# Sums of four heads' exponentials in one matmul of 228 columns instead of four of 57

## The chip, the cores and the metric

One Trainium2 chip, one of its cores. The metric is device time in microseconds (us). Several runs are quoted as a median with their lowest and highest value.

## The reference

Two attention blocks read the same input `x` (2048 positions, 1024 features, 32 heads of 32), and a gate mixes them. The change touches only block B, a sliding attention over eight positions, two apart:

```python
W, dil = 8, 2
idx = pos[:, None] - off[None, :]            # off = 0, 2, ..., 14
logits = einsum("bhsd,bhswd->bhsw", q, kg) * scale   # masked where idx < 0
attn = softmax(logits, axis=-1)
o = einsum("bhsw,bhswd->bhsd", attn, vg)     # then @ wo
```

Block A (a linear attention) and the projections of both blocks are most of the work.

## The kernel before

The kernel splits the positions into even and odd ones, so a window becomes eight neighbours. It then works in 18 *fills*. A fill holds two blocks (h = 0, 1) of `nq` = 57 queries (56 in the last fill of each half) with 64 keys each, for all 32 heads. A fill has three parts on TensorE and around it:

- **S**: 64 small matmuls give the scores of 32 heads, 64 keys x 57 queries each. ScalarE takes exp of all of them, VectorE multiplies by a mask, into `E`. `E` has 64 keys of each block on 64 partitions, and its columns are ordered by head: 57 for each.
- **PV**: two groups (g = 0, 1) of 16 heads. Each head's 64 values (64 x 32) are multiplied by its exponentials, and a 64 x 32 block of ones is multiplied by the same exponentials to give the sum of each query, repeated on 32 partitions.
- ScalarE takes Ln and Exp(-x) of the sums, VectorE multiplies.

The array of 128 x 128 is used as eight tiles of 64 x 32: `tile_position=(64 * h, 32 * j)`.

```python
def each(e, g=g):                       # one PV group: 64 matmuls
    for o in range(2):                  # 0: values, 1: sums
        for c in range(4):
            for h in range(2):
                for j in range(4):
                    hd = 16 * g + 4 * c + j
                    w = vt[64*h:64*h+64, hd*32:hd*32+32] if o == 0 else ones[64*h:64*h+64, :]
                    last = e.matmul(SO[2*g+h].ap((4*o+c)*nq, (4*o+c+1)*nq)[32*j:32*j+32, :], w,
                                    E[64*h:64*h+64, (8*j+4*g+c)*nq:(8*j+4*g+c+1)*nq],
                                    start=True, stop=True, tile_position=(64*h, 32*j))
    return last
P.op("pe", each, 0.35, mode="c", ...)   # 0.35: the planner's cost, in us
# ... then Ln, Exp(-x) on ScalarE and the product on VectorE, for this g
```

Each `e.matmul` becomes two instructions, a weight load and a matmul; I call them a *pair*. Each `P.op` is one step of a plan. A list scheduler orders all steps when the kernel is built, from the costs given; the last instruction of a step signals a semaphore. A column index of `E` and of the sums in PSUM shows the opening: for fixed j and g the four heads c = 0..3 lie side by side in both.

Of the kernel before, what the change touches and what calls it, by code (L numbers as in the profile page):

```python
# [1102 lines left out]
def build_kernel(nc, A_x, A_wqkv, A_wo, B_x, B_wqkv, B_wo, gate_w, out):  # L1103
# [10 lines left out]
    def SB(shape, dtype, name, at=None):  # L1114
        n = SZ[dtype]
        for d in shape[1:]:
            n *= d
        if at is None:
            at = base[0]
            base[0] += (n + 31) // 32 * 32  # L1120
        uid[0] += 1
        h = nc.alloc_sbuf_tensor_at("%s_%d" % (name, uid[0]), list(shape), dtype, offset=at)
        return Tile("S", h, at, list(shape), dtype)
# [35 lines left out]
    def hb(p0, p1, half):  # L1159
        return [("H%d" % half, p0, p1, None)]  # L1160

    xT = SB([128, 8, S], BF16, "xT")
    qT = SB([128, 8, S], BF16, "qT")
    kT = SB([128, 8, S], BF16, "kT")
# [3 lines left out]
    ones = SB([128, 32], BF16, "ones")  # L1168
# [7 lines left out]
    g = SB([128, NT], F32, "g")  # L1176
# [46 lines left out]
    def plan(seen):  # L1223

        P = Prog(nc, nc.alloc_semaphore)
# [94 lines left out]
        def group(bank, lhs, rhs, reads, lo=0, hi=8):  # L1320
            def fn(e):
                last = None
                for dc in range(lo, hi):
                    last = e.matmul(bank.ap(), lhs(dc), rhs(dc), start=(dc == 0), stop=(dc == 7))  # L1324
                return last
            return P.op("pe", fn, (hi - lo) * mm(512), reads=reads, writes=[bank.iv])
# [19 lines left out]
        def w_half(slot, half):  # L1346
            return (lambda dc: ws[slot][:, dc, half * 512:half * 512 + 512]), ws[slot].part((0, 8), (half * 512, half * 512 + 512))

        def w_cols(slot, j):
            return (lambda dc: ws[slot][:, dc, j * 128:(j + 1) * 128]), ws[slot].part((0, 8), (j * 128, (j + 1) * 128))  # L1350
# [17 lines left out]
        for t, half in [(4 * b + i, half) for b in range(NT // 4) for half in range(2) for i in range(4)]:  # L1368
            vt, vs = vst.next()
            xs, xr = x_tile(t)  # L1370
            bank = main.next()
            w, wr = w_half(0, half)
            step = 2 if t == 0 else 8
            for d in range(0, 8, step):
                o = group(bank, xs, w, [xr, ws[0].part((d, d + step), (half * 512, half * 512 + 512))], d, d + step)
            move(vt[:, :], bank.ap, 512, bank, vt.all())
            P.op("sp", lambda e, t=t, vt=vt, half=half: e.dma_start(vB_hbm[t * 128:(t + 1) * 128, half * 512:half * 512 + 512], vt[:, :]), 0.6, reads=[vt.all()],
                 writes=[hb(t * 128, (t + 1) * 128, half)], chan="vst%d" % vs, lat=0.5, prio=5)
# [29 lines left out]
        SO = banks[4:8]  # L1408
# [5 lines left out]
        def fill(e_, qs, nq, offs):  # L1414
            t0 = e_ * HS
            k0 = [qs + nq * h - offs[h] for h in range(2)]
            m = msk[KINDS.index((nq, offs))]
            vt, vslot = vr.next()
            for h in range(2):
                P.op("sp", lambda e, h=h: e.dma_start(vt[64 * h:64 * h + 64, :], vB_hbm[t0 + k0[h]:t0 + k0[h] + 64, :]), 0.4,  # L1420
                     reads=[hb(t0 + k0[h], t0 + k0[h] + 64, i) for i in range(2)], writes=[vt.all()], chan="v%d_%d" % (vslot, h), lat=0.5)

            def s_fn(e):
                for c in range(8):
                    for h in range(2):
                        for j in range(4):
                            last = e.matmul(SO[j].ap(c * nq, (c + 1) * nq)[64 * h:64 * h + 64, :], kT[32 * j:32 * j + 32, c, t0 + k0[h]:t0 + k0[h] + 64],  # L1427
                                            qT[32 * j:32 * j + 32, c, t0 + qs + h * nq:t0 + qs + (h + 1) * nq], start=True, stop=True, tile_position=(32 * j, 64 * h))
                return last
            P.op("pe", s_fn, 0.45, mode="r", reads=[kT.part((0, 8), (t0 + k0[0], t0 + k0[1] + 64)), qT.part((0, 8), (t0 + qs, t0 + qs + 2 * nq))],  # L1430
                 writes=[s.iv for s in SO], name="S")
            E, _ = Er.next()
            P.op("act", lambda e: e.activation(E[:, 0:32 * nq].rearrange("p (j q) -> p j q", j=4), ps[:, 4:8, 0:8 * nq], ACT.Exp), act(32 * nq),  # L1433
                 reads=[s.iv for s in SO], writes=[E.all()])
            ev = lambda: E[:, 0:32 * nq].rearrange("p (g q) -> p g q", g=16)
            P.op("dve", lambda e: e.tensor_tensor(ev(), ev(), m[:, :, :].rearrange("p r q -> p (r q)")[:, None, :].to_broadcast([128, 16, 2 * nq]), ALU.mult),
                 0.15 + 32 * nq / 1920.0, reads=[E.all(), m.all()], writes=[E.all()])

            def values():

                for g in range(2):
                    def each(e, g=g):
                        for o in range(2):
                            for c in range(4):
                                for h in range(2):
                                    for j in range(4):
                                        hd = 16 * g + 4 * c + j
                                        w = vt[64 * h:64 * h + 64, hd * 32:hd * 32 + 32] if o == 0 else ones[64 * h:64 * h + 64, :]
                                        last = e.matmul(SO[2 * g + h].ap((4 * o + c) * nq, (4 * o + c + 1) * nq)[32 * j:32 * j + 32, :], w,  # L1449
                                                        E[64 * h:64 * h + 64, (8 * j + 4 * g + c) * nq:(8 * j + 4 * g + c + 1) * nq],  # L1450
                                                        start=True, stop=True, tile_position=(64 * h, 32 * j))
                        return last
                    bi = [SO[2 * g].iv, SO[2 * g + 1].iv]
                    P.op("pe", each, 0.35, mode="c", reads=[vt.all(), ones.all(), E.all()], writes=bi, name="PV")
                    L, _ = Lr.next()
                    pb = lambda o, g=g: ps[:, 4 + 2 * g:6 + 2 * g, 4 * o * nq:4 * (o + 1) * nq]
                    P.op("act", lambda e, L=L, pb=pb: e.activation(L[:, :, 0:4 * nq], pb(1), ACT.Ln), act(8 * nq), reads=bi, writes=[L.all()])
                    P.op("act", lambda e, L=L: e.activation(L[:, :, 0:4 * nq], L[:, :, 0:4 * nq], ACT.Exp, scale=-1.0), act(8 * nq), reads=[L.all()], writes=[L.all()])  # L1458
                    P.op("dve", lambda e, L=L, pb=pb, g=g: e.tensor_tensor(  # L1459
                        qT[:, 4 * g:4 * g + 4, t0 + qs:t0 + qs + 2 * nq].rearrange("p c (h q) -> p h c q", h=2),  # L1460
                        pb(0).rearrange("p h (c q) -> p h c q", c=4), L[:, :, 0:4 * nq].rearrange("p h (c q) -> p h c q", c=4), ALU.mult), dps(8 * nq),
                        reads=bi + [L.all()], writes=[qT.part((4 * g, 4 * g + 4), (t0 + qs, t0 + qs + 2 * nq))])
            after(PVLAG, values)

        pace = [0.0]
# [3 lines left out]
        def slot(rate):  # L1469
            slot_n[0] += 1  # L1470
            while later and later[0][0] <= slot_n[0]:
                later.pop(0)[1]()
            while states and states[0][0] <= slot_n[0]:
                states.pop(0)[1]()
            pace[0] = min(pace[0] + rate, 1.0) if todo else 0.0
            if todo and pace[0] >= 1.0:
                pace[0] -= 1.0
                fill(*todo.pop(0))

        def after(n, f, cols=False):  # L1480
            later.append((slot_n[0] + n, f, cols))
            later.sort(key=lambda x: x[0])


        for e_ in range(2):
            if True:
                for j in range(8):
                    for isq in range(2):
                        for u in (2 * e_, 2 * e_ + 1):
                            bank = main.next()  # L1490
                            w, wr = w_cols(1 + isq, j)
# [38 lines left out]
        for t in range(NT):  # L1530
# [3 lines left out]
            for r in range(4):  # L1534
                bank = main.next()
                w, wr = w_half((3, 0)[r // 2], r % 2)
# [126 lines left out]
        for t in range(NT):  # L1663
            tgt, c0 = a_loc(t)
            o_, os_ = osb.next()
            e_, r = t // 8, t % 8
            parts = [(0, 512), (512, 1024)] if t < NT - 1 else [(0, 512), (512, 768), (768, 1024)]
            for f0, f1 in parts:
# [3 lines left out]
                def fn(e, t=t, bank=bank, f0=f0, f1=f1):  # L1672
# [8 lines left out]
                    reads=[bank.iv, gm.all(), tgt.part((i0, i1), (c0, c0 + 128))], writes=[o_.part((f0, f1))])  # L1681
                if t == NT - 1 or f1 == 1024:
                    c = f0 if t == NT - 1 else 0
                    P.op("sp", lambda e, e_=e_, r=r, o_=o_, c=c, f1=f1: e.dma_start(out2[e_, r * 128:(r + 1) * 128, c:f1], o_[:, c:f1]), 0.5,
                         reads=[o_.part((c, f1))], chan="out%d_%d" % (os_, c), lat=1.0)
# [13 lines left out]
    P, flag_op = best[:2]  # L1699
# [52 lines left out]
```

## Time and profile before

| | before |
|---|---|
| time, median (lowest to highest) | 510.26 us (509.35 to 511.56), 3 runs |
| span of the profiled run | 507.9 us |
| PE busy | 501.5 us, 99% |
| matmuls / weight loads | 6121 / 6121 |

The busy times of the profile's page (us, share of the span, number of instructions; PE is TensorE's matmuls, PEld its weight loads), of the kernel before:

```profile
PE 501.5 (99%) x6121; PEld 239.4 (47%) x6121; DVE 265.0 (52%) x456; ACT 196.2 (39%) x335; POOL 6.6 (1%) x30
```

The chain that ended last, from the same page, as shares of the span, first by engine and then by line:

```profile
PE 96%; SPq 2%; DMA 1%; ACT 1%; issue 0%; DVE 0%
PE ps_all L1324 75%; PE ps_all L1674 11%; PE ps_all L1449 4%; PE ps_all L1427 2%; PE ps_all L1599 1%; SPq L1294 1%; DMA w_4_52<-in_B_wqkv_dram 1%; PE ps_all L1520 1%; PE ps_all L1577 1%; SPq L1299 0%; PE ps_all L1392 0%; ACT ra_50_98 L1601 0%; ACT ra_52_100 L1601 0%; ACT ra_51_99 L1601 0%; ACT e_27_75 L1333 0%
```

TensorE bounds the kernel: 96% of the chain is its own work. Line 1324 holds the projections, 1449 PV, 1427 S.

Pieces of the chain in order of time (start, length, what; PEq and SPq are the sequencers of TensorE and SyncE, *issue* is time in which an engine waited for nothing that the profile shows), around the first fill:

```profile
127.89 0.63 PE ps_all L1427 x64
128.52 5.29 PE ps_all L1324 x24
133.81 1.17 PE ps_all L1449 x128
134.97 3.56 PE ps_all L1324 x16
```

S, then 24 matmuls of projections, then the 128 matmuls of PV without a break, then projections. The neighbours change from fill to fill, but each of the 18 has its 128 PV matmuls in one unbroken run.

Weight loads in order of time (start, length, engine, line, operands, array rows * columns, count) in the same PV.

```profile
133.74 0.19 PEld L1449 LDWEIGHTS ps_all<-E_39_87,v_43_91 64*32 64x32 bf16 x32 [0.42 <-DVE mx_55_103 L1280]
133.87 0.44 PEld L1449 LDWEIGHTS ps_all<-E_39_87,ones_58 64*32 64x32 bf16 x32
134.22 0.35 PEld L1449 LDWEIGHTS ps_all<-E_39_87,v_43_91 64*32 64x32 bf16 x32
134.52 0.35 PEld L1449 LDWEIGHTS ps_all<-E_39_87,ones_58 64*32 64x32 bf16 x32
134.90 0.76 PEld L1324 LDWEIGHTS ps_all<-xT_49,w_5_53 128*128 128x128 bf16 x5
```

A fill's PV takes from 133.74 to 134.90, the first weight load of the next projection: 1.16 us (1.166 us as the mean of 18 fills, from the single records). In the single records the steady step from one pair to the next is 8.33 ns. "S" takes 0.632 us by the same measure.

The gate, line 1392, is the one place in this kernel with wide matmuls on several tiles (durations in ns, least/median/most):

```profile
L1392 PE MATMUL ps_all<-xT_49,gwr_67 x32: 379/379/390, 62.0 to 63.5; 128*32 128x512 bf16 x32
```

32 of these fit into 1.84 us of the chain, so four tiles work at once: 57 ns a matmul, against 216 ns from one projection matmul of 512 columns to the next.

### The profile page before, as it was taken

What the parts mean: (1) busy time and instruction counts of PE and PEld (TensorE: products, weight loads), DVE (VectorE), ACT (ScalarE), POOL (GpSimd) and SP (SyncE); (2) the same over time, 40 slices, a digit from 0 to 9 for tenths busy, and PEclk for the clock granted to TensorE, in tenths of its full rate; (3) what the DMA queues carried; (4) which work ended last, traced back from release to release, by engine and by line L of the source; (5) the groups of instructions that cost most, each with busy time, mean ns of one, the idle gap of its engine ahead of it and who ended that gap; (6) DMA issues with size and microseconds to landing.
All of it is one profiled execution on the core that took longest, in us unless ns stands there. A gap on an engine that the chain in (4) does not pass through costs nothing.

```text
span 507.9 us, 13377 instructions
## 1 busy us (share of the span) xinstructions
PE 501.5 (99%) x6121; PEld 239.4 (47%) x6121; DVE 265.0 (52%) x456; ACT 196.2 (39%) x335; POOL 6.6 (1%) x30
## 2 busy tenths in 40 slices
PE   8999999999999999999999999999999999999996
PEld 3444444444555555555555555544444444444443
DVE  3112245655667675554555555488776673334443
ACT  1111111111444454655565465479965453110000
POOL 5000000000000000000000000000000000000000
PEclk9999999999999999999999999999999999999999
DMA  8999980000033060100010100500000000002212
GB/s 227 198 209 320 352 248 1 1 0 1 24 104 109 23 199 24 35 25 23 23 35 23 35 3 4 168 0 0 1 1 1 1 1 0 3 29 76 83 74 76
DMA packets 47417, 35.04 MB, mean 69 GB/s; under 512 B 22261, under 2 KB 43125, under 8 KB 47354
## 3 DMA queue, kind: packets, MB, share of 16 engines
q1 hardware_dynamic: 46810, 33.59, 23.2%
q8 instruction: 50, 0.82, 0.7%
q10 hardware_dynamic: 544, 0.52, 0.3%
q14 instruction: 13, 0.11, 0.1%
HBM read 21.51 MB, written 8.40 MB: 59 GB/s over the span
## 4 chain that ended last, share of the span: by engine, by line
PE 96%; SPq 2%; DMA 1%; ACT 1%; issue 0%; DVE 0%
PE ps_all L1324 75%; PE ps_all L1674 11%; PE ps_all L1449 4%; PE ps_all L1427 2%; PE ps_all L1599 1%; SPq L1294 1%; DMA w_4_52<-in_B_wqkv_dram 1%; PE ps_all L1520 1%; PE ps_all L1577 1%; SPq L1299 0%; PE ps_all L1392 0%; ACT ra_50_98 L1601 0%; ACT ra_52_100 L1601 0%; ACT ra_51_99 L1601 0%; ACT e_27_75 L1333 0%
## 5 line engine op out<-in xcount | busy, mean ns | idle before, releaser
L1324 PE MATMUL ps_all<-xT_49,w_6_54 128*128 128x512 bf16 x512 | 118.1, 379 | 0.1
L1324 PE MATMUL ps_all<-w_4_52,xT_49 128*128 128x512 bf16 x512 | 116.0, 379 | 0.7 <-DMA xT_49<-in_A_x_dram 0.7
L1324 PEld LDWEIGHTS ps_all<-xT_49,w_6_54 128*128 128x128 bf16 x512 | 49.5, 98 | 59.2 <-ACT ra_52_100 L1601 0.6
L1324 PEld LDWEIGHTS ps_all<-w_4_52,xT_49 128*128 128x128 bf16 x512 | 48.3, 98 | 59.4 <-DMA xT_49<-in_A_x_dram 2.1
L1324 PE MATMUL ps_all<-w_7_55,xT_49 128*128 128x512 bf16 x256 | 59.3, 379 | 0.0
L1324 PE MATMUL ps_all<-xT_49,w_5_53 128*128 128x512 bf16 x256 | 58.4, 379 | 0.0
L1674 PE MATMUL ps_all<-w_7_55,qT_50 128*128 128x512 bf16 (+1 forms) x264 | 55.4, 373 | 0.0
L1324 PE MATMUL ps_all<-w_5_53,xT_49 128*128 128x512 bf16 x192 | 42.7, 379 | 0.0
L1674 PEld LDWEIGHTS ps_all<-w_7_55,qT_50 128*128 128x128 bf16 x264 | 25.8, 98 | 29.7
L1324 PEld LDWEIGHTS ps_all<-xT_49,w_5_53 128*128 128x128 bf16 x256 | 24.5, 98 | 29.2 <-issue 0.4
L1324 PEld LDWEIGHTS ps_all<-w_7_55,xT_49 128*128 128x128 bf16 x256 | 24.1, 98 | 28.0 <-issue 0.3
L1324 PEld LDWEIGHTS ps_all<-w_5_53,xT_49 128*128 128x128 bf16 x192 | 18.8, 98 | 22.6
L1359 ACT ACTIVATE qT_50<-ps_all 128x512 bf16<-128x512 f32 x15 | 9.0, 597 | 37.1 <-PE ps_all L1324 37.1
L1356 ACT ACTIVATE kT_51<-ps_all 128x512 bf16<-128x512 f32 x14 | 8.4, 597 | 35.5 <-PE ps_all L1324 35.5
L1358 DVE TENSOR_SCALAR xT_49<-ps_all,g_65 128x512 bf16<-128x512 f32 x15 | 11.2, 749 | 19.9 <-PE ps_all L1324 19.9
L1280 DVE TENSOR_TENSOR mx_54_102<-mx_54_102,kT_51 128x1024 bf16<-128x1024 bf16 x16 | 11.1, 691 | 16.9 <-ACT kT_51 L1356 16.9
L1280 DVE TENSOR_TENSOR mx_54_102<-mx_54_102,qT_50 128x1024 bf16<-128x1024 bf16 x16 | 11.1, 691 | 16.8 <-ACT qT_50 L1359 16.7
L1459 DVE TENSOR_TENSOR qT_50<-ps_all,L_41_89 128x456 bf16<-128x456 f32 (+1 forms) x18 | 11.3, 628 | 11.6 <-ACT L_41_89 L1458 11.6
L1355 DVE CAST kT_51<-ps_all 128x512 bf16<-128x512 f32 x18 | 12.3, 684 | 7.6 <-PE ps_all L1324 7.6
L1433 ACT ACTIVATE E_39_87<-ps_all 128x1824 bf16<-128x1824 f32 (+1 forms) x9 | 15.2, 1688 | 2.3 <-PE ps_all L1427 1.8
L1433 ACT ACTIVATE E_40_88<-ps_all 128x1824 bf16<-128x1824 f32 (+1 forms) x9 | 15.2, 1688 | 0.6
L1324 PE MATMUL ps_all<-w_5_53,pq_8_56 128*128 128x512 bf16 x64 | 15.1, 379 | 0.0
(179 smaller groups left out, 518.8 us busy)
## 6 DMA issues: line engine op xcount, KB each, us to landing
w_5_53<-in_B_wqkv_dram SPq DMA_DIRECT2D x2, 1024.0 KB, 7.8
w_6_54<-in_B_wqkv_dram SPq DMA_DIRECT2D x2, 1024.0 KB, 8.5
w_4_52<-in_A_wqkv_dram SPq DMA_DIRECT2D x2, 1024.0 KB, 9.3
w_7_55<-in_A_wqkv_dram SPq DMA_DIRECT2D x2, 1024.0 KB, 8.2
w_5_53<-in_A_wo_dram SPq DMA_DIRECT2D x2, 1024.0 KB, 5.6
w_6_54<-in_A_wqkv_dram SPq DMA_DIRECT2D x2, 1024.0 KB, 5.4
w_7_55<-in_B_wo_dram SPq DMA_DIRECT2D x2, 1024.0 KB, 5.9
out_dram<-o_60_108 SPq DMA_DIRECT2D x8, 256.0 KB, 2.0
```

Source lines behind the costliest of these rows:

```text
L1280: P.op("dve", lambda e, m=m, op=op: e.tensor_tensor(m[:, 0:n], m[:, 0:n], src, op), 0.08 + n / 1920.0, reads=[m.all(), reg], writes=[m.all()],
L1294: return P.op("sp", lambda e: e.dma_start_transpose(xT[:, :, t * 128:(t + 1) * 128], x2[e_, r * 128:(r + 1) * 128, :]), 1.5, writes=[xT.pa ...
L1324: last = e.matmul(bank.ap(), lhs(dc), rhs(dc), start=(dc == 0), stop=(dc == 7))
L1355: fd = lambda e: e.tensor_copy(dst, src())
L1356: fa = lambda e: e.activation(dst, src(), ACT.Copy)
L1358: fd = lambda e: e.tensor_scalar(dst, src(), scale, None, op0=ALU.mult)
L1359: fa = lambda e: e.activation(dst, src(), ACT.Copy, scale=scale)
L1427: last = e.matmul(SO[j].ap(c * nq, (c + 1) * nq)[64 * h:64 * h + 64, :], kT[32 * j:32 * j + 32, c, t0 + k0[h]:t0 + k0[h] + 64], qT[32 * j: ...
L1433: P.op("act", lambda e: e.activation(E[:, 0:32 * nq].rearrange("p (j q) -> p j q", j=4), ps[:, 4:8, 0:8 * nq], ACT.Exp), act(32 * nq), rea ...
L1449: last = e.matmul(SO[2 * g + h].ap((4 * o + c) * nq, (4 * o + c + 1) * nq)[32 * j:32 * j + 32, :], w, E[64 * h:64 * h + 64, (8 * j + 4 * g ...
L1459: P.op("dve", lambda e, L=L, pb=pb, g=g: e.tensor_tensor(qT[:, 4 * g:4 * g + 4, t0 + qs:t0 + qs + 2 * nq].rearrange("p c (h q) -> p h c q" ...
L1674: last = e.matmul(bank.ap(0, f1 - f0), qT[:, dc, t * 128:(t + 1) * 128], ws[3][:, dc, f0:f1], start=(dc == 0), stop=(dc == 7))
```

## The change

The intent: the weights of the sums are the same block of ones for all heads, and the four heads of a tile are neighbours in `E` and in PSUM. So one matmul of 4 x 57 = 228 columns can stand for four. A group has 40 pairs instead of 64. Two costs of the planner change with it.

```diff
-            P.op("pe", s_fn, 0.45, mode="r", ...)
+            P.op("pe", s_fn, 0.55, mode="r", ...)
 ...
                     def each(e, g=g):
-                        for o in range(2):
-                            for c in range(4):
-                                for h in range(2):
-                                    for j in range(4):
-                                        ...            # values if o == 0, else ones: 57 columns
+                        for c in range(4):
+                            for h in range(2):
+                                for j in range(4):
+                                    ...                # values, 57 columns, as before
+                        for h in range(2):
+                            for j in range(4):
+                                last = e.matmul(SO[2*g+h].ap(4*nq, 8*nq)[32*j:32*j+32, :], ones[64*h:64*h+64, :],
+                                                E[64*h:64*h+64, (8*j+4*g)*nq:(8*j+4*g+4)*nq],
+                                                start=True, stop=True, tile_position=(64*h, 32*j))
                         return last
-                    P.op("pe", each, 0.35, mode="c", ...)
+                    P.op("pe", each, 0.36, mode="c", ...)
```

## The prediction

> **What bounds the kernel.** TensorE. The page has PE busy 99% of a 507.9 us span, and the chain of waits is PE for 96%. In the table of windows PE is busy for 99.6 to 100% of every stretch from 14.8 to 448 us. Projections (line 1324) are 75% of the chain; the changed line, 1449 (PV), is 4.1%, line 1427 (S) 2.2%. PE time taken out of PV comes off the span unless the re-planned order gives it back.
>
> **What PV costs now.** The chain in order of time shows 18 fills, each an unbroken run of 128 PV matmuls (two groups of 64): 1.17 us from the first matmul to the next projection matmul, 21.0 us in all. In the single records the steady spacing is 8.33 ns per pair of weight load and matmul, although one matmul lasts 194 ns: the tiles overlap. A projection matmul of 512 columns starts every 215.5 ns, 0.42 ns a column, so 57 columns stream for 24 ns, and each of the 8 tiles gets a matmul every 67 ns. PV is bound by the number of instructions, not by columns. After the last PV matmul 0.126 us pass before the next projection.
>
> **What the change does.** Columns per tile stay (4 x 57 = 228). Of a group's 32 pairs for sums 24 go: 48 per fill, 864 in all. ScalarE's and VectorE's work is the same.
> - Taken out: 48 x 8.33 = 0.40 us per fill.
> - Added: a wide matmul streams 228 x 0.42 = 96 ns. The eight are issued in 67 ns, so group 1's first matmul on tile 0 may wait up to 30 ns (the queue can hide it). The drain after the fill is 171 x 0.42 = 72 ns longer.
> - Net: 0.30 to 0.33 us per fill, 5.3 to 5.9 us in all, on the critical path.
>
> This needs the eight wide matmuls to stream at once. The Trainium skill's "TensorEngine Tiling (Array Packing)", section Key Properties, says that different tiles execute in parallel. The trace agrees for four column tiles: the gate (line 1392) does 32 matmuls of 512 columns in 1.84 us, 57 ns each against 215 ns. For eight tiles kept busy no record proves it. If only four ran at once, about 3.4 us of the gain would go (36 x 96 ns).
>
> **The plan.** A list scheduler orders the kernel from costs, and two change (S 0.45 to 0.55, PV 0.35 to 0.36). Neighbours may move: how often PV stands beside a kv group of its tiling mode (saving a drain of about 0.1 us), and the ScalarE-bound holes at 350 to 353 us. I allow 2 us either way.
>
> **Time.** 510.26 - 5.7, about 504.6 us, range 501.9 to 507.4 (8 in 10). Faster by over 2% (under 500.1) 0.04; within 2% 0.93; slower by over 2% 0.03.
>
> **What would show it.** PE falls by 864 to about 5257 matmuls and as many weight loads. In the chain a fill's PV takes 0.82 to 0.88 us (80 matmuls) instead of 1.17; its share falls to about 3%. Short PV matmuls keep 194 ns, wide ones last about 265 ns; spacing stays 8.33 ns. The drain after PV grows from 0.126 to about 0.2 us. S stays 0.63 us. ScalarE and VectorE stay at 196 and 265 us busy. Projections keep 215.5 ns.
>
> **What would make it wrong.** Wide matmuls not overlapping on eight tiles (a fill stays near 1.0 us or more); the queue stalling on a busy tile for longer than its streaming; a new plan that puts bubbles on PE around ScalarE's exponentials, or removes those at 350 us; a lower granted clock.

## More of the kernel before

Busy time by stretch (start:end, length, then PE, PEld, VectorE, ScalarE and GpSimd with counts, the granted clock, the share of the DMA engines, GB/s). I cut at the first weight load of S, and where, after the last fill, the first weights that are not a projection's are loaded:

```profile
0.00:127.82 127.82, 125.82 (x593) 55.47 (x593) 48.88 (x82) 22.78 (x37) 6.64 (x30) 1.00 0.58 155
127.82:333.12 205.30, 205.30 (x4729) 106.09 (x4728) 120.19 (x211) 106.30 (x158) 0.00 (x0) 1.00 0.17 53
333.12:507.90 174.78, 170.38 (x802) 77.81 (x800) 95.94 (x165) 67.09 (x140) 0.00 (x0) 1.00 0.07 25
```

The *stage of the fills* is 205.30 us long and PE is busy in all of it. I use its length below, because the part before it, with the first loads, varies from run to run (127.6 to 129.3 us in the traces told here), and the stage does not feel that.

All runs told here were in the fast state, at a granted TensorE clock of 0.998 to 1.000.

## The result and the profile after

| | before | after |
|---|---|---|
| time, median (lowest to highest) | 509.85 us (509.35 to 511.56), 4 runs | 504.41 us (504.26 to 504.77), 4 runs |
| ratio | 1 | 0.9889, 95% interval 0.9864 to 0.9913 |
| a fill's PV, mean of 18 | 1.166 us | 0.864 us |
| gap from its last weight load to the next projection's | 0.128 us | 0.198 us |
| S of a fill | 0.632 us | 0.633 us |
| stage of the fills | 205.30 us | 199.90 us |

A ratio is the mean time of one kernel's fast runs over that of the other's of the same rounds, so it is not quite the ratio of the medians quoted. The change is a gain of 1.1%, and its interval excludes 1.

The page of after, busy times:

```profile
PE 488.4 (97%) x5190; PEld 232.7 (46%) x5257; DVE 264.5 (53%) x456; ACT 192.9 (38%) x335; POOL 6.6 (1%) x30
```

There are 5257 weight loads, 864 fewer than before, as many as pairs were taken out. But only 5190 matmuls are recorded. 67 records are missing, in this trace and in none of the other twelve, so PE's fall of 13 us busy time says nothing. The same kernel was run once more at the end (k_after), and that trace is complete:

```profile
PE 495.7 (99%) x5257; PEld 232.7 (46%) x5257; DVE 264.6 (53%) x456; ACT 192.9 (38%) x335; POOL 6.6 (1%) x30
```

There PE's busy time is 5.8 us below that of before. The chain of the first trace shows where its records are missing:

```profile
PE 95%; issue 2%; DMA 1%; ACT 1%; SPq 0%; DVE 0%
PE ps_all L1324 76%; PE ps_all L1677 11%; PE ps_all L1427 2%; PE ps_all L1447 2%; PE ps_all L1602 1%; PE ps_all L1452 1%; DMA xT<-in_A_x_dram 1%; PE ps_all L1523 1%; PE ps_all L1580 1%; ACT ra L1604 0%; PE ps_all L1392 0%; SPq L1294 0%; SPq L1299 0%; ACT e L1333 0%; ACT ra L1605 0%
```

```profile
128.48 0.63 PE ps_all L1427 x64
129.11 0.16 issue
129.27 5.13 PE ps_all L1324 x23
134.40 0.24 PE ps_all L1447 x32
...
135.26 0.16 issue
135.42 3.40 PE ps_all L1324 x15
```

After S there is a piece "issue" of 0.16 us and then 23 projection matmuls where before there were 24. The first matmul after S is not recorded, and after PV it is the same (15 instead of 16). Whoever measures a fill from its first matmul to the next recorded one finds 1.09 us there and misses most of the gain. The weight loads are complete:

```profile
134.33 0.19 PEld L1447 LDWEIGHTS ps_all<-E,v 64*32 64x32 bf16 x32 [0.42 <-DVE mx L1280]
134.46 0.24 PEld L1452 LDWEIGHTS ps_all<-E,ones 64*32 64x32 bf16 x8
134.62 0.37 PEld L1447 LDWEIGHTS ps_all<-E,v 64*32 64x32 bf16 x32
134.94 0.15 PEld L1452 LDWEIGHTS ps_all<-E,ones 64*32 64x32 bf16 x8
135.19 0.33 PEld L1324 LDWEIGHTS ps_all<-xT,w 128*128 128x128 bf16 x3
```

From 134.33 to 135.19: 0.86 us instead of 1.16. The wide weight loads and matmuls by their line:

```profile
L1452 PEld LDWEIGHTS ps_all<-E,ones x288: 87/89/91, 134.5 to 315.5; 64*32 64x32 bf16 x144
L1452 PE MATMUL ps_all<-E,ones x288: 252/266/267, 134.6 to 315.5; 64*32 64x228 bf16 x128, 64*32 64x224 bf16 x16
```

A wide matmul lasts 266 ns in the median, a short one 190 (195 in before). The profile records when a matmul starts and models when it ends, so these lengths are modelled. The stretches:

```profile
0.00:128.41 128.41, 124.94 (x582) 55.56 (x593) 48.77 (x82) 22.78 (x37) 6.63 (x30) 1.00 0.58 154
128.41:328.31 199.90, 193.88 (x3825) 99.36 (x3865) 119.79 (x211) 103.13 (x158) 0.00 (x0) 1.00 0.18 54
328.31:503.00 174.69, 169.54 (x786) 77.75 (x800) 95.94 (x165) 67.03 (x140) 0.00 (x0) 1.00 0.07 25
```

The stage of the fills is 5.40 us shorter. 18 x (1.166 - 0.864) us is 5.44 us. What stands before it and after it is within 0.6 and 0.1 us of before. Within 0.04 us the stage's whole difference is PV. ScalarE's busy time fell too, by 3 us with the same 335 instructions. It did not get less work: the lengths of its records add up to 210.5 us in before and to 210.8 in after; more of them overlap, and busy time counts an overlap once.

### The profile page after: what moved, and what is told of

Its sections match the earlier page's. It is cut to its first block, busy times and chain, and to the rows that moved or that the text cites. A ratio compares the mean times of both kernels' runs of the same rounds, so it can differ in the third digit from the quotient of the medians.

```text
span 503.0 us, 11582 instructions
## 1 busy us (share of the span) xinstructions
PE 488.4 (97%) x5190; PEld 232.7 (46%) x5257; DVE 264.5 (53%) x456; ACT 192.9 (38%) x335; POOL 6.6 (1%) x30
## 4 chain that ended last, share of the span: by engine, by line
PE 95%; issue 2%; DMA 1%; ACT 1%; SPq 0%; DVE 0%
PE ps_all L1324 76%; PE ps_all L1677 11%; PE ps_all L1427 2%; PE ps_all L1447 2%; PE ps_all L1602 1%; PE ps_all L1452 1%; DMA xT<-in_A_x_dram 1%; PE ps_all L1523 1%; PE ps_all L1580 1%; ACT ra L1604 0%; PE ps_all L1392 0%; SPq L1294 0%; SPq L1299 0%; ACT e L1333 0%; ACT ra L1605 0%
## 5 line engine op out<-in xcount | busy, mean ns | idle before, releaser
L1324 PE MATMUL ps_all<-w,xT 128*128 128x512 bf16 x922 | 207.7, 379 | 6.3 <-issue 4.0
L1324 PE MATMUL ps_all<-xT,w 128*128 128x512 bf16 x747 | 169.3, 379 | 2.5 <-issue 1.9
L1324 PEld LDWEIGHTS ps_all<-w,xT 128*128 128x128 bf16 x960 | 91.3, 98 | 110.9 <-issue 2.3
L1324 PEld LDWEIGHTS ps_all<-xT,w 128*128 128x128 bf16 x768 | 73.9, 98 | 88.8 <-ACT ra L1604 0.6
L1677 PE MATMUL ps_all<-w,qT 128*128 128x512 bf16 (+1 forms) x259 | 55.2, 373 | 0.3
L1677 PEld LDWEIGHTS ps_all<-w,qT 128*128 128x128 bf16 x264 | 25.8, 98 | 29.7
L1433 ACT ACTIVATE E<-ps_all 128x1824 bf16<-128x1824 f32 (+1 forms) x18 | 30.4, 1687 | 3.1 <-PE ps_all L1427 2.0
L1331 ACT ACTIVATE e<-ps_all 128x512 bf16<-128x512 f32 x32 | 19.1, 598 | 31.5 <-PE ps_all L1324 30.7
L1333 ACT ACTIVATE e<-ps_all 128x512 bf16<-128x512 f32 x32 | 19.2, 601 | 29.3 <-PE ps_all L1324 27.8
L1337 DVE SCALAR_TENSOR_TENSOR pk<-ps_all,e 128x512 bf16<-128x512 f32 x32 | 22.0, 689 | 0.8
L1604 ACT ACTIVATE ra<-ps_all,eps 128x512 f32<-128x512 f32 x32 | 21.5, 688 | 2.2 <-PE ps_all L1602 2.0
```

The source lines that it names most:

```text
L1324: last = e.matmul(bank.ap(), lhs(dc), rhs(dc), start=(dc == 0), stop=(dc == 7))
L1331: P.op("act", lambda e: e.activation(e_[:, :], bank.ap(), ACT.Exp), act(512), reads=[bank.iv], writes=[e_.all()])
L1333: P.op("act", lambda e: e.activation(e_[:, :], bank.ap(), ACT.Exp, accum_out=qe[:, col:col + 1]), act(512) + 0.1, reads=[bank.iv], writes= ...
L1337: P.op("dve", lambda e: e.scalar_tensor_tensor(out=dst, in0=bank.ap(), scalar=0.0, in1=e_[:, :], op0=ALU.max, op1=ALU.add), dps(512), read ...
L1433: P.op("act", lambda e: e.activation(E[:, 0:32 * nq].rearrange("p (j q) -> p j q", j=4), ps[:, 4:8, 0:8 * nq], ACT.Exp), act(32 * nq), rea ...
L1604: P.op("act", lambda e: e.activation(R[:, :], db.ap(), ACT.Ln, bias=eps[:, :]), act(512), reads=[db.iv, eps.all()], writes=[R.all()])
```

## The experiments

The theory before the runs (A): PV is bound by the number of pairs, 8.33 ns each; the price of the change is a longer *drain* (the gap from a fill's last weight load to the next projection's) and a short wait on busy tiles. Rivals: (B) the columns streamed set the time; (C) the gain comes from the two costs and the new plan.

For each run, beside the time, I give the mean length of a fill's PV and the length of the stage of the fills, both from weight loads.

| run | median us | ratio to before, 95% interval | fill us | stage us |
|---|---|---|---|---|
| before (profiled) | 510.26 | | 1.166 | 205.30 |
| after | 504.41 | 0.9889 (0.9864 to 0.9913) | 0.864 | 199.90 |
| a_oldcosts | 504.96 | 0.9899 (0.9879 to 0.9920) | 0.862 | 199.89 |
| b_newcosts | 510.20 | 1.0006 (0.9985 to 1.0027) | 1.168 | 205.36 |
| c_half | 505.40 | 0.9910 (0.9893 to 0.9927) | 0.922 | 200.93 |
| d_widefirst | 504.01 | 0.9884 (0.9862 to 0.9906) | 0.838 | 199.45 |
| e_narrowv | 510.49 | 1.0000 (0.9975 to 1.0026) | 1.146 | 204.97 |
| f_double | 507.84 | 0.9953 (0.9931 to 0.9975) | 1.057 | 203.42 |
| g_sametile | 511.42 | 1.0020 (0.9997 to 1.0044) | 1.247 | 206.77 |
| h_spread | 503.21 | 0.9868 (0.9846 to 0.9890) | 0.793 | 198.58 |
| i_burst | 502.72 | 0.9872 (0.9857 to 0.9888) | 0.766 | 198.19 |
| j_oneop | 501.93 | 0.9849 (0.9836 to 0.9862) | 0.742 | 197.58 |
| k_after | 504.80 | 0.9912 (0.9899 to 0.9926) | 0.864 | 199.89 |

### a_oldcosts and b_newcosts: the matmuls without the costs, and the costs without the matmuls

```diff
 a_oldcosts, against after:          b_newcosts, against before:
-  P.op("pe", s_fn, 0.55, ...)      -  P.op("pe", s_fn, 0.45, ...)
+  P.op("pe", s_fn, 0.45, ...)      +  P.op("pe", s_fn, 0.55, ...)
-  P.op("pe", each, 0.36, ...)      -  P.op("pe", each, 0.35, ...)
+  P.op("pe", each, 0.35, ...)      +  P.op("pe", each, 0.36, ...)
```

> The kernel after with the two planner costs of before (S 0.45, PV 0.35): the matmuls change, the costs do not. Theory A (PV is bound by the number of load-and-matmul pairs, 8.33 ns each): 504.4 us within 0.8, a fill of PV 0.864 us as in after. Rival C (the gain comes from the new plan that the new costs give): close to before, 509 us or more.

> The kernel before with the two planner costs of after (S 0.55, PV 0.36): the costs change, the matmuls do not. Theory A: 509.9 us within 0.8, a fill of PV 1.166 us. Rival C: close to after, 505 us or less.

The stage of the fills is 199.89 us with the new matmuls and old costs, and 205.36 us with the old matmuls and new costs. The costs and the plan that follows from them are worth less than 0.1 us of the stage. Rival C falls. (The order of TensorE's instructions does change in a few places with the costs; it costs and gains nothing.)

### c_half: half the dose

```diff
-  one wide matmul of 4 * nq columns for each (h, j)
+  for c in (0, 2): one matmul of 2 * nq columns for each (h, j)
```

> Half the dose: the sums of two heads in one matmul of 114 columns, 16 of them in a group (96 pairs in a fill instead of 80 or 128; columns unchanged). Theory A: the pairs take 32 x 8.33 = 0.267 us less than in before; the drain after the fill is 57 columns x 0.42 ns = 0.024 us longer; a fill takes about 0.92 us and the kernel 505.5 us. Rival B (streaming of columns bounds PV and the gain has another source) has no reason for a value between: it gives the time of before or of after.

A fill takes 0.922 us and the kernel 505.40 us, both as expected. The gap after the fill is 0.150 us, between 0.128 (57 columns last) and 0.198 (228 columns last): it grows by the streaming time of the columns of the last matmul.

### e_narrowv: half of the matmuls with few columns

```diff
 before, in the loop:
+  n = 8 if o == 0 else nq
-  ... SO[...].ap((4*o+c)*nq, (4*o+c+1)*nq) ..., E[..., (8*j+4*g+c)*nq:(8*j+4*g+c+1)*nq]
+  ... SO[...].ap((4*o+c)*nq, (4*o+c)*nq + n) ..., E[..., (8*j+4*g+c)*nq:(8*j+4*g+c)*nq + n]
```

> The kernel before, all 128 pairs of a fill kept, but the 64 short matmuls with values stream 8 columns instead of 57 (wrong result on purpose). Theory A (number of pairs): a fill stays at 1.166 us within 0.02, the kernel at 509.8 us within 0.8. Rival B (columns streamed set the time of PV): 43% of the columns are gone, a fill would fall towards 0.7 us and the kernel towards 502 us.

The result is wrong. A fill takes 1.146 us: 43% of the columns are gone and 2% of the time. Rival B falls, and with c_half and after this shows A: the pairs count. No run takes out a weight load and leaves its matmul, so whether the load, the matmul or both set the 8.33 ns stays open. The 20 ns that did go are explained further down. The first and the last line of the weight loads of the first fill, the three between left out:

```profile
135.23 0.19 PEld L1450 LDWEIGHTS ps_all<-E,v 64*32 64x32 bf16 x32 [0.42 <-DVE mx L1280]
136.38 0.55 PEld L1324 LDWEIGHTS ps_all<-xT,w 128*128 128x128 bf16 x4
```

### f_double: do eight tiles really stream at once?

```diff
+  for rep in range(2):
       for h in range(2):
           for j in range(4):
               last = e.matmul(... 4 * nq columns ...)
```

> The kernel after with the eight wide matmuls of each group given twice in a row (same values written again, right result). All eight tiles stream at once: the second matmul on a tile can start about 100 ns after the first (67 ns if only the issue counted), so each group grows by about 0.10 us, a fill to 1.06 us, the kernel to about 508 us. Only four tiles at once: a group grows by 0.19 us or more, the kernel to about 511.5 us.

Weight loads of the first fill:

```profile
133.90 0.19 PEld L1447 LDWEIGHTS ps_all<-E,v 64*32 64x32 bf16 x32 [0.42 <-DVE mx L1280]
134.02 0.31 PEld L1453 LDWEIGHTS ps_all<-E,ones 64*32 64x32 bf16 x16
...
134.95 0.55 PEld L1324 LDWEIGHTS ps_all<-xT,w 128*128 128x128 bf16 x4
```

A fill takes 1.057 us and the kernel 507.84 us, as expected for eight tiles at once. In the single records the first matmul of the second eight starts 96 ns after the first of the first eight in the first group, and 106 ns in the second (means of 18 fills). 228 columns at 0.42 ns are 96 ns, and with only four tiles at once it would be 192, so tiles hardly slow each other here. It also shows the limit: eight wide matmuls need 96 ns of streaming but only 67 ns of issue, so with wide matmuls alone the columns would bind.

### d_widefirst: the wide matmuls ahead of the short ones

```diff
 after, in each group:
-  32 short matmuls, then 8 wide
+  8 wide, then 32 short
```

> The kernel after with the eight wide matmuls of a group ahead of its 32 short ones, the same plan. Theory A with the drain as the one loss: the last matmul of a fill is short again, the drain goes back from 0.198 to 0.128 us, a fill takes 0.79 to 0.80 us, the kernel 503.2 us. Rival: the longer gap after the fill belongs to the whole fill (wide matmuls still streaming on other tiles, or weights queued), not to the last matmul: gap stays 0.2 us, 504.4 us. A third outcome: short matmuls waiting on busy tiles at the start of the fill eat the gain.

The third outcome came. The gap after the fill went back to 0.128 us, as the theory says. But the part before it grew from 0.666 to 0.710 us, so of 70 ns a fill 44 were lost again. The weight loads show where:

```profile
133.56 0.11 PEld L1445 LDWEIGHTS ps_all<-E,ones 64*32 64x32 bf16 x8 [0.42 <-DVE mx L1280]
133.59 0.41 PEld L1452 LDWEIGHTS ps_all<-E,v 64*32 64x32 bf16 x32
133.92 0.15 PEld L1445 LDWEIGHTS ps_all<-E,ones 64*32 64x32 bf16 x8
133.99 0.37 PEld L1452 LDWEIGHTS ps_all<-E,v 64*32 64x32 bf16 x32
134.40 1.19 PEld L1324 LDWEIGHTS ps_all<-xT,w 128*128 128x128 bf16 x7
```

In after, the 41st weight load of a fill starts 0.289 us after the first, here 0.359 us. In every kernel a fill starts with a fast burst of some 32 pairs (3.7 ns each in the mean of after), then pauses, then goes on at 8.33 ns. Here the pause ends 70 ns later, although the wide matmuls are only eight of the burst. At this point I took this for waiting on busy tiles. (Such a wait is in the trace: the burst breaks off for 61 ns ahead of its 17th load, the third on its tile. But at the end of the burst only 33 ns of it are left, and the 70 ns have the reason given under h_spread.)

### g_sametile: one tile after the other

```diff
 after, the sums of a group:
-  for h, j: one wide matmul
+  for h, j: for c in range(4): one matmul of 57 columns
```

> The sums as in before in number and size (32 matmuls of 57 columns in a group), but the four of a tile are given one after the other instead of going round the eight tiles; costs of after. If only the number of instructions counts: a fill takes 1.166 us, 509.8 us. If a tile must finish one matmul before the next, and issue is in order, each of them takes at least its 24 ns of streaming: a group's sums take 0.64 us or more instead of 0.27, a fill 1.9 us or more, the kernel 522 us or more.

A miss of the expectation: a fill takes 1.247 us, not 1.9 or more. Only 0.08 us more than in before. The matmuls (line 1447 values, 1453 sums), at the change from the first to the second group:

```profile
134.37 0.45 PE L1453 MATMUL ps_all<-E,ones 64*32 64x57 bf16 x28
134.63 0.19 PE L1447 MATMUL ps_all<-E,v 64*32 64x57 bf16 x1
134.63 0.19 PE L1453 MATMUL ps_all<-E,ones 64*32 64x57 bf16 x1
134.64 0.20 PE L1447 MATMUL ps_all<-E,v 64*32 64x57 bf16 x2
134.66 0.19 PE L1453 MATMUL ps_all<-E,ones 64*32 64x57 bf16 x2
134.66 0.22 PE L1447 MATMUL ps_all<-E,v 64*32 64x57 bf16 x4
134.69 0.19 PE L1453 MATMUL ps_all<-E,ones 64*32 64x57 bf16 x1
134.72 0.40 PE L1447 MATMUL ps_all<-E,v 64*32 64x57 bf16 x25
```

In the program all 32 sums of the first group stand ahead of the values of the second. In the trace values start while sums still wait for their tile. So a matmul that waits for its tile does not stop those behind it that go to another tile. In the single records the 32 sums take about 8.3 ns each, although four in a row share a tile. That speaks against "waiting on busy tiles" as the reason for what d_widefirst lost.

### h_spread: wide matmuls spaced so that no tile is asked for too early

`V(h, c)` is four short matmuls on the four tiles of row half h, `W(h)` four wide ones.

```diff
 group 0:
-  V(0,0) V(1,0) V(0,1) V(1,1) V(0,2) V(1,2) V(0,3) V(1,3) W(0) W(1)
+  V(0,0) V(1,0) V(0,1) V(1,1) V(0,2) V(1,2) V(0,3) W(0) V(1,3) W(1)
 group 1:
-  V(0,0) V(1,0) V(0,1) V(1,1) V(0,2) V(1,2) V(0,3) V(1,3) W(0) W(1)
+  V(0,0) V(0,1) V(1,0) W(0) V(1,1) W(1) V(0,2) V(0,3) V(1,2) V(1,3)
```

> The same 80 matmuls of after in another order: every wide matmul has at least 12 pairs (100 ns) before the next matmul on its tile, the first 28 matmuls of a fill are short, and the last 20 are short. By the reasons found so far neither the stall after the first wide block (28 ns) nor the longer drain (70 ns) is left: a fill takes 0.77 us, the kernel about 502.7 us. If the stalls are not a matter of busy tiles: 504 us as before.

Half a miss. The gap after the fill is 0.128 us: the 70 ns came back. But the part before the gap is 0.665 us, no shorter than the 0.666 us of after, so the 26 ns that I had put down to busy tiles are still there: a fill takes 0.793 us, not 0.77. In the single records there are two steps of 34 ns where others are 8.33, at places 69 and 72 of the 80. (Places count the pairs of a fill from 0. The last 16 matmuls are short, not 20 as the expectation has it; this changes nothing here.)

Setting such places side by side gave a theory (Q): *an instruction can be issued only when the one some 64 places earlier, 32 pairs, has finished.* In detail:

- The burst has some 32 pairs in all kernels and then pauses until the first matmuls end. In e_narrowv these stream 49 columns fewer, 20 ns, and the fill is 20 ns shorter. In d_widefirst they stream 171 more, 72 ns, and the pause ends 70 ns later.
- In the steady part, 32 pairs take 32 x 8.33 = 267 ns. A short matmul (194 ns) is done by then, a wide one (266 ns) is just late. In after the extra steps (23 and 19 ns) stand 32 pairs behind the first wide matmul, in h_spread (34 ns) 32 pairs behind the second wide block.
- The last matmul of group 0, which signals the semaphore, stands at place 39 of 80 here and at 63 of 128 in before. A step of 34 ns stands at 72 and at 96: 32 pairs lie between. It stands at the corresponding place in after and d_widefirst (72), f_double (80) and g_sametile (96).

The Trainium skill, "TensorE: Matmul & The Clock Gate", gives 64 as TensorE's queue depth in its opening table. The burst of 32 pairs agrees with it. That a place comes free only when its instruction ends is what the runs suggest; the page does not say it. The kept traces hold a strict check: from the profile's end of a matmul to the start of the matmul 32 pairs later (in order of their starts) there are never less than 26 ns, in any fill of the 13 traces. After each pause, and behind the wide matmuls that hold something up, it is 26 to 28 ns, whether the matmul has 8, 57 or 228 columns. Two further runs put the theory to the test.

### i_burst: the wide matmuls of group 0 into the burst

```diff
 h_spread, group 0:
-  ... V(0,3) W(0) V(1,3) W(1)
+  ... W(0) W(1) V(0,3) V(1,3)
```

> As h_spread, but in the first group the eight wide matmuls stand at places 24 to 31 of the fill, ahead of the last eight short ones, instead of at 28 to 31 and 36 to 39. Theory Q, formed from the runs so far: a pair can be issued only when the instruction 64 places (32 pairs) earlier has finished; a wide matmul lasts 266 ns, as long as 32 pairs at 8.33 ns, so it holds up the pair 32 places later by about 26 ns when it stands in the steady part of a group (h_spread: place 36 to 39, the stall seen at place 69), but not when it is issued in the fast burst of the first 32 pairs, followed by the pause. So the stall at 69 goes: a fill takes 0.767 us instead of 0.793, the kernel 502.7 us. If the stall at 69 has to do with busy tiles in the second group, which is the same as in h_spread, it stays: 0.793 us, 503.2 us.

A fill takes 0.766 us and the step at 69 is gone; the kernel takes 502.72 us. Group 1 is the same as in h_spread, so busy tiles in it were not the cause. (By time alone the two runs cannot be told apart, 0.9868 and 0.9872 with overlapping intervals; the traces decide.)

### j_oneop: one step and one signal for both groups

```diff
 i_burst:
-  P.op("pe", each, 0.36, mode="c", ..., writes=bi, name="PV")       # for each g
+  if g == 0:
+      P.op("pe", lambda e, f=each: (f(e, 0), f(e, 1))[1], 0.72, mode="c", ..., writes=[s.iv for s in SO], name="PV")
```

> As i_burst, but both groups of a fill are one step of the plan: one semaphore signal at the end instead of one after each group, ScalarE starts on the first group only after both. In every run so far there is a stall of 34 ns (26 more than a step) exactly 32 pairs after the last matmul of the first group, the one that signals. Theory Q (a signalling matmul finishes later and holds up the pair 32 places on): the stall goes, a fill takes 0.741 us, the stage of the fills is 0.47 us shorter, kernel 502.2 us. If the stall is a matter of the instruction stream and not of the signal, it stays at 0.767 us. A plan with ScalarE's work later could cost something elsewhere.

Weight loads of the first fill:

```profile
133.66 0.17 PEld L1446 LDWEIGHTS ps_all<-E,v 64*32 64x32 bf16 x24 [0.42 <-DVE mx L1280]
...
134.15 0.21 PEld L1446 LDWEIGHTS ps_all<-E,v 64*32 64x32 bf16 x16
134.40 1.19 PEld L1324 LDWEIGHTS ps_all<-xT,w 128*128 128x128 bf16 x7
```

From 133.66 to 134.40: 0.742 us as the mean, as expected. The step of 34 ns is gone, so it belonged to the signal in the middle of the fill: in the traces of before, after, h_spread and i_burst the signal is all that stands between the groups, with no wait and no other TensorE instruction. That a signalling matmul *finishes later*, as the expectation says, is not shown: the step is 34 ns where that matmul is short (before, i_burst) and where it is wide and ends some 70 ns later (after, h_spread), which looks more like a fixed cost of 26 ns. The kernel takes 501.93 us. The new plan also moved four instructions from ScalarE to VectorE (331 and 460 instead of 335 and 456). No cost elsewhere can be seen: the rest after the stage is 174.8 us, as in before.

### k_after: after once more

```diff
 (no edit)
```

> The kernel after itself, unchanged, on the same chip and in the same rounds as the last two versions, to compare them with it: 504.4 us within 0.6, a fill 0.864 us.

504.80 us and a fill of 0.864 us, as expected. In the same rounds j_oneop has a ratio to before of 0.9849 (0.9836 to 0.9862) and after one of 0.9912 (0.9899 to 0.9926): j_oneop beats both kernels. It has the right result. The same kernel had 0.9889 in the earlier rounds: a difference of 0.2% between runs of different rounds is noise. The length of the stage, 199.90 and 199.89 us, repeats far better.

## Why the prediction was right

- **What bounds PV**: right. The number of pairs, shown by e_narrowv (few columns, same time), c_half (half the pairs, as predicted) and after.
- **0.40 us taken out of a fill**: right. 48 x 8.33 ns is 0.400 us. 1.038 us from the first to the last weight load became 0.666: 0.372 us, because 28 ns were given back inside the fill.
- **A drain longer by 72 ns**: right. 0.128 became 0.198 us, and d_widefirst and h_spread got it back by putting short matmuls last.
- **Up to 30 ns lost on tile 0 between the groups**: right in size by luck, wrong in cause. The wait on the tile is there: in after, group 1's first matmul starts 34 ns after its weight load, where others of the steady part start after 4. But the weight loads go on at 8.33 ns, so the queue hid it, as the prediction allowed. The 26 ns that were lost stand at places 65 and 66. h_spread left room on every tile and did not get them back; i_burst did, by moving the wide matmuls of group 0 to where the pair 32 places on is not held up. By theory Q what was lost is time in TensorE's queue behind long matmuls; the prediction had no such term.
- **Eight tiles at once**: right, and shown by f_double, where a tile takes its next wide matmul after 96 to 106 ns.
- **The plan, 2 us either way**: right that it might do nothing, far too wide: a_oldcosts and b_newcosts put it under 0.1 us of the stage. One reason that I gave is wrong: a kv group next to PV does not save the drain. The gap after PV is 0.128 us in before whether projections or kv follow, and 0.198 us in after.
- **Signs in the profile**: 5257 weight loads, a fill of 0.864 us (0.82 to 0.88 predicted), a share of 3% for the two PV lines, wide matmuls of 266 ns, S and the projections (216 ns) unchanged: all found. The 5257 matmul records were found in k_after's trace; in the first one 67 are missing. Not found: ScalarE's busy time of 196 us (193, because more of its records overlap).
- **Time**: 504.6 predicted, 504.41 measured. Of the gain, 5.44 us are 18 fills at 0.302 us. That the total came out so close is partly luck: the 0.302 us hold a loss that the prediction put elsewhere, and the before of the same rounds was 509.85 us, not the 510.26 that the prediction started from.

## What to carry to other kernels

When small matmuls on tiles start one after the other at a steady pace, far shorter than they last, and the pace does not change with their columns, count instructions: merging matmuls with the same weights into a wider one takes out pairs at that pace until the streaming of the columns binds. Put the wide matmuls where short ones follow: not at the end of a run before matmuls of another tile shape (a gap of 0.198 us instead of 0.128 here), and rather in the burst at the start than in the steady part, where a block of them held up the pairs 32 places later. Look at weight loads as well as at matmuls before believing a gap: records of matmuls can be missing at the very places that you measure.

## What the Trainium skill lacked or had wrong

- "TensorE: Matmul & The Clock Gate", Part 1: says that the start of one matmul to the start of the next never drops below about 25 ns. On eight tiles it is 8.33 ns steady, with a weight load for each, and about 3.7 ns in the burst at the start of a fill. The page's own Part 3 gives about 4 ns between starts on different tiles, which fits the burst; the steady 8.33 ns stands in neither part.
- The same page, Part 3: says that matmuls start and end strictly in program order. In g_sametile matmuls of the second group start before sums of the first that stand ahead of them in the program and wait for their tile, in each of the 18 fills. (Ends are modelled, so the trace says nothing of their order.)
- The same page, opening table: gives the queue depth of 64. It lacks what follows from it here: a matmul of 266 ns or a signalling one holds up the pair 32 places later by about 26 ns (h_spread, i_burst, j_oneop: 0.793, 0.766, 0.742 us a fill). Part 3 does have a term of 26.3 ns for each semaphore increment, close to the signal's 26 ns, but in the tail behind the last matmul and not 32 pairs on.
- "TensorEngine Tiling (Array Packing)", Instruction Overhead: says a matmul of one column has the same latency as one of 60. The profile's lengths differ, 173 ns with 8 columns and 195 with 57 (modelled, but the pause at the start of a fill is 20 ns shorter too). The pace is the same for both, 8.33 ns. The 60 cycles that it gives as the overhead of each matmul are not what a stream on eight tiles pays: at one column a cycle (0.42 ns here) they would be 25 ns, an estimate from the page's figure, three times the pace.
- No page that I read says that TensorE's matmul records can be missing while its weight-load records are complete, or where: 67 of 5257 in one trace of 13, among them the first matmul after each run of S.
